# Linear attention beside a SiLU feed-forward: another trigger for one input load, and another order of four transfers and two matmul blocks

## The chip, the cores and the metric

The kernel runs on one core of a Trainium2 chip. The metric is the device time of one execution in microseconds (us). TensorE does the matmuls, VectorE (DVE in the profile), ScalarE (ACT) and GpSimd (POOL) the elementwise work, SyncE (SP) issues most of the transfers. PSUM, which matmuls write, has eight banks of 512 fp32 columns.

## The reference

One input x of 2048 tokens and 448 channels is normalised. Two branches read the result, and both are added to x.

```python
xn  = layernorm(x)                                    # over 448 channels, eps 1e-5
q, k, v = split(xn @ wqkv)                            # 16 heads of 28
pq, pk  = q @ w_phi, k @ w_phi                        # per head, 28 x 28
phi = lambda p: concat(softmax(p), softmax(-p))       # 56 features per head
kv, z = phi(pk).T @ v, sum(phi(pk), tokens)
o   = phi(pq) @ kv / (phi(pq) @ z + 1e-6)
out = x + o @ wo + silu(xn @ w1) @ w2                 # w1: 448 x 1792, w2: 1792 x 448
```

All inputs are bfloat16.

## The kernel before

**Tiles.** The tokens are 16 tiles of 128. `x_sb` holds x, `RA` the normalised rows (`xn_sb`), and `xnT` their transposes, channels on the partitions. The 448 channels are four pieces of 128 that overlap in part; dense blocks multiply 64 rows at a time, two such matmuls side by side.

**Recording and ordering.** The function does not emit instructions at once. Each operation is recorded with its engine, what it reads and writes, and a name (`_Prog.op`, line 186); the reads and writes give its dependencies. `_Prog.schedule` (line 228) then lays the operations out one engine after the other by estimated times, and `emit_engine` (line 1209) writes each engine's program in that order, with semaphore waits for the dependencies that cross engines. Two things fix orders by hand: `chain(names)` (line 1022) makes every named operation follow the one before it on its engine, and the string `PLAN` (line 361) gives the order of TensorE's blocks.

**The words of PLAN.** `aF5@4` is the first half of layer 1 (ffn1) block 5 in the PSUM banks 4 and 5, `bF5` its second half, after which ScalarE writes silu of the two banks to `hT`. `av4@6` and `bv4` are the halves of the value products of tiles 4 and 5 (`v_block`, line 795); after the second half ScalarE copies the two banks to `vaug`. Blocks F0 to F6 are those of tokens 0 to 511, F7 to F13 of tokens 512 to 1023 (tiles 4 to 7), and so on. `f0@6` and `f1@6` fold `w_phi` into the key weights (`fold_k`, line 672), `ak2`, `bk2` are key products of tiles 2 and 3. A second half also waits until the first half has left TensorE, since both add to the same banks.

**The head.** Tiles 0 to 3 are normalised and transposed on the engines: VectorE's statistics (lines 708, 709), ScalarE's square root (712), VectorE's reciprocal (714) and normalisation (723), TensorE's transposes (541), and copies out of PSUM (547, 551). Tiles 0 and 1 are loaded by SyncE, one DMA each; tiles 2 and 3 by one DMA of ScalarE, which is recorded as `x2`. It reads nothing that another engine makes; line 1036 makes it wait for an operation of GpSimd:

```python
byname["x2"].deps.add(byname["ident"].id)
```

Behind it on ScalarE follow, by the chain in line 1034, a warm activation with its table load and the square roots. GpSimd's first operations are, in order, `ones`, `epst`, `ident` (the identity for the transposes), `neghalf`, `ones4`, the zero fill of `Wp` (the first operation with the name `wp_zero`), a mask, the zero fill of `Wp0` (the second), and more masks and fills. TensorE meanwhile runs 39 matmuls on constants (line 591).

**SyncE's queue.** From tile 4 on a pair of tiles is transposed by one DMA, from `RA` to `xnT` (`xnT_dma5` for tiles 4 and 5, `xnT_dma7` for 6 and 7, and so on, line 731); it waits for VectorE's normalisation of both. Nine further DMA transposes (`wT_dma0` to `wT_dma8`, line 650) bring pieces of `wqkv`; `f0` and `f1` read the pieces 4 to 8. `x8` and `x12` load tiles 8 to 11 and 12 to 15. SyncE issues in order, by the chain in line 1072, so an issue that waits holds back all behind it.

Of the kernel before, what the change touches and what calls it, by code (L numbers as in the profile page):

```python
# [140 lines left out]
class _Prog:  # L141
# [86 lines left out]
    def schedule(self, stalls=()):  # L228
# [53 lines left out]
        while done < n:  # L282
# [75 lines left out]
TAIL = {"act": 110.0, "dve": 85.0, "pool": 45.0}  # L358
SIGNAL = {("act", "pe"): 60.0, ("act", "dve"): 40.0, ("dve", "pe"): 100.0, ("dve", "sp"): 30.0, ("dve", "dve"): 34.0,
          ("pool", "pe"): 100.0}  # L360
PLAN = """r0 aF3@4 r2 r1 bF3 aF6@0 aF4@6 bF6 bF4 aF5@4 av2@2 av0@0 bv2 bF5 bv0 av4@6 aF10@2 bv4 aF9@0 bF10 f0@6 bF9 aF12@4 aF7@2
aF11@0 f1@6 bF11 bF7 bF12 aF8@0 ak2@6 bF8 bk2 av12@2 av8@4 ak0@0 bv8 bv12 bk0 av10@6 aF22@4 bv10 bF22 aF17@2 aF14@0 av14@6
bF17 bv14 aF18@4 bF14 aF27@6 ak4@2 bF27 bF18 bk4 ak6@0 av6@6 ak8@4 bv6 bk8 bk6 ak12@2 aF25@6 bk12 bF25 aY0@45 aY0 aF21@0
aF23@2 bF21 ak14@6 bF23 bY0 g0@1 bk14 bY0 aF13@0 aF19@2 bF13 aF24@6 aF20@4 bF19 bF20 bF24 ak10@0 g1@3 bk10 K0 K6 K4 K12
# [6 lines left out]
def bass_parallel_sum__linear_kernel_hedgehog__dense_activation_silu__prompt_kernel(  # L371
# [37 lines left out]
    with es:  # L409
        def sb(name, shape, dt):  # L410
            return es.enter_context(nc.sbuf_tensor(name, shape, dt))
# [60 lines left out]
        ident = sb("ident", [128, 128], BF16)  # L472
# [33 lines left out]
        P = _Prog()  # L506
# [83 lines left out]
        for i in range(39):  # L590
            o = P.op("pe", 107.0, lambda e: e.matmul(banks[3][:, 0:128], unit, unit, start=True, stop=True),
                 reads=[], writes=[banks[3][:, 0:128]], name="warm", mode=128)
# [306 lines left out]

        early = {int(w[2]) for w in PLAN.split() if w[1:2] == "Y"}  # L900
        ob_cnt = [0]
# [120 lines left out]
        def chain(names):  # L1022
            byname = {o.name: o for o in P.ops}
            for a, b in zip(names, names[1:]):
                byname[b].odeps.add(byname[a].id)
                byname[b].odeps -= byname[b].deps
# [6 lines left out]
        chain("bnst0 bnag0 bnst1 rstd0 bnag1 xn0 rstd1 xn1 bnst2 bnag2 bnst3 rstd2 xn2 bnag3 rstd3 xn3 ev3".split())  # L1033
        chain("x2 warm_act ve0 ve1 ev0a ev0 ev1a ve2 ev1 ve3 ev2a ev2 silu_table".split())
        byname = {o.name: o for o in P.ops}
        byname["x2"].deps.add(byname["ident"].id)
        byname["x2"].xfer, byname["x2"].lat = 0.0, 2800.0
        fold_loads()

# [29 lines left out]

        for t in range(8, NT):  # L1070
            ln_tile(t)
        chain("x8 wT_dma4 wT_dma5 wT_dma6 x12 wT_dma7 xnT_dma5 xnT_dma7 wT_dma8 xnT_dma9 xnT_dma11 xnT_dma13 xnT_dma15 wT_dma0 wT_dma1 wT_dma2 wT_dma3 w2 "
              "wo0 wor0 wo1 wor1".split())
        memset(phq[:, :, :, KP:128], 0.0, 400, "phq0")
        for t in (0, NEK):
# [28 lines left out]

        for word in PLAN.split():
            n0 = len(P.ops)
# [81 lines left out]
        for e in ("pe", "act", "dve", "pool"):  # L1188
            cnt = 0
            for oid in order[e]:  # L1190
                o = ops[oid]
# [4 lines left out]
        for e in ENGINES:  # L1196
            for oid in order[e]:
                o = ops[oid]
# [76 lines left out]
```

## Time and profile before

| | |
|---|---|
| median of three runs | 144.99 us (144.57, 144.99, 145.91) |
| profiled execution | 145.19 us, of which the span of instructions is 143.9 us |
| granted TensorE clock, mean | 1.0 |
| TensorE busy | 140.4 us in 1969 matmuls |
| VectorE, ScalarE, GpSimd busy | 90.3, 79.7 and 75.3 us |
| moved by DMA | 17.59 MB in 45,044 packets, mean 122 GB/s |

The span is the time from the first to the last instruction of the program; the profiled execution's time holds 1.3 us around it. Times within the profile count from the span's start. The profile's page gives busy times, the span in 40 slices of 3.6 us, and the chain of work that ended last; the timeline lists instructions in order of time with start and duration, where several of one kind are merged into one row. "L524" is line 524 of the kernel, the helper that records every matmul, so matmuls are told apart by their tiles; `phT` is also the place where w1 lies at first, so `psum<-xnT,phT` is a layer 1 matmul, `psum<-wv,xnT` a value product, and `psum<-BD,wT` or `psum<-BD,Y_sb` a fold (the transposed weight pieces lie in `Y_sb` and `wT8`). Rows with a q behind the engine ("ACTq", "SPq") are DMAs that it issues, with the time that the issue took, not the transfer.

### The profile page before, as it was taken

To read this page: it belongs to the slowest core of one execution; us is meant where nothing else is said; L and a number is where in the kernel's file an instruction comes from. 1 tells how busy PE (TensorE), PEld (TensorE's weight loads), DVE (VectorE), ACT (ScalarE), POOL (GpSimd) and SP (SyncE) were. 2 spreads that over 40 slices of the span, in tenths; PEclk is the share of its full clock that TensorE was granted. 3 is DMA by queue.
4 is the path that set the end of the run, shared out by engine and by line. 5 is a ranking of instruction groups with operands and counts; after the bars stand their busy time and mean duration, and the time that the engine had idled before them with its cause. 6 is when DMAs were issued, how large, how long until landed. Compare 5 with 4: busy or idle time off the path is not lost.

```text
span 143.9 us, 4560 instructions
## 1 busy us (share of the span) xinstructions
PE 140.4 (98%) x1969; PEld 83.1 (58%) x1969; DVE 90.3 (63%) x194; ACT 79.7 (55%) x98; POOL 75.3 (52%) x95
## 2 busy tenths in 40 slices
PE   7799999999999999999999999999999999999994
PEld 7794444445444544477677656555555556555773
DVE  1879897700760069939049999957977564265533
ACT  4577866479996999889787949237440000000000
POOL 8808667430196008799944999993495700000000
PEclk9999999999999999999999999999999999999999
DMA  4999999555990000000000058959789998825422
GB/s 129 315 324 300 270 191 97 100 106 82 322 328 8 0 2 5 0 0 5 0 5 5 0 98 168 143 110 108 152 158 146 234 214 151 141 40 112 162 95 64
DMA packets 45044, 17.59 MB, mean 122 GB/s; under 512 B 36944, under 2 KB 44640, under 8 KB 45024
## 3 DMA queue, kind: packets, MB, share of 16 engines
q1 hardware_dynamic: 42448, 15.25, 53.3%
q10 hardware_dynamic: 2448, 2.02, 5.0%
q8 instruction: 15, 0.25, 0.7%
q0 software_dynamic: 128, 0.03, 0.1%
q14 instruction: 5, 0.04, 0.1%
HBM read 6.57 MB, written 1.84 MB: 58 GB/s over the span
## 4 chain that ended last, share of the span: by engine, by line
PE 94%; DMA 2%; DVE 1%; SPq 0%; ACT 0%; issue 0%
PE psum L524 94%; DMA x_sb<-in_A_x_dram 2%; PE psum L541 1%; DVE st L708 0%; SPq L561 0%; DVE RA L723 0%; DVE x_sb L1009 0%; ACT ve L712 0%; DVE rstd L714 0%; DVE mv L709 0%
## 5 line engine op out<-in xcount | busy, mean ns | idle before, releaser
L524 PE MATMUL psum<-xnT,phT 64*128 64x512 bf16 (+1 forms) x428 | 46.6, 350 | 0.0
L524 PE MATMUL psum<-w_sb,hT 64*128 64x448 bf16 (+4 forms) x455 | 46.0, 341 | 0.0
L843 DVE TENSOR_REDUCE Rec<-Ek_sb 128x32 f32<-128x896 bf16 (+1 forms) x20 | 24.6, 1257 | 18.6 <-ACT Ek_sb L547 18.6
L524 PEld LDWEIGHTS psum<-w_sb,hT 64*128 64x128 bf16 (+1 forms) x455 | 23.8, 94 | 17.2 <-issue 0.2
L547 ACT ACTIVATE hT<-psum 128x1024 bf16<-128x1024 f32 x28 | 27.6, 1024 | 10.8 <-PE psum L524 10.8
L524 PEld LDWEIGHTS psum<-xnT,phT 64*128 64x128 bf16 (+1 forms) x428 | 22.6, 95 | 17.6 <-ACT vaug L547 0.7
L880 POOL TENSOR_TENSOR RA<-Ek_sb,Rec 128x896 bf16<-128x896 bf16 x16 | 27.0, 1723 | 6.0 <-DVE Rec L844 4.4
L524 PE MATMUL psum<-Wqk,xnT 64*128 64x432 bf16 x224 | 24.4, 343 | 0.0
L547 ACT ACTIVATE Ek_sb<-psum 128x864 bf16<-128x864 f32 x24 | 20.4, 916 | 6.4 <-PE psum L524 5.5
L853 POOL TENSOR_TENSOR Ek_sb<-Ek_sb,Rec 128x896 bf16<-128x896 bf16 x8 | 13.4, 1698 | 16.3 <-DVE Rec L844 16.3
L524 PEld LDWEIGHTS psum<-Wqk,xnT 64*128 64x128 bf16 x224 | 11.1, 94 | 8.2 <-ACT hT L547 0.4
L547 ACT ACT_TABLE_LOAD x11 | 14.1, 1283 | 2.7 <-POOL Wp L554 1.8
L853 POOL TENSOR_TENSOR phT<-phT,Rec 128x896 bf16<-128x896 bf16 x8 | 13.4, 1699 | 1.7 <-issue 0.9
L524 PE MATMUL psum<-wv,xnT 64*128 64x448 bf16 x112 | 12.4, 349 | 0.0
L708 DVE BATCH_NORM_STATS2 st<-x_sb 128x6 f32<-128x448 bf16 x16 | 9.7, 604 | 3.5 <-DMA x_sb<-in_A_x_dram 3.5
L524 PE MATMUL psum<-wo_sb,vaug 64*128 64x448 bf16 (+2 forms) x102 | 11.3, 338 | 0.0
L1009 DVE TENSOR_TENSOR x_sb<-psum,x_sb 128x448 bf16<-128x448 f32 (+2 forms) x13 | 7.2, 583 | 5.5 <-PE psum L524 5.5
L988 DVE TENSOR_TENSOR vaug<-psum,rden 128x448 bf16<-128x448 f32 x16 | 9.3, 620 | 0.0
L723 DVE TENSOR_SCALAR RA<-x_sb,mv,rstd 128x384 bf16<-128x384 bf16 (+2 forms) x28 | 8.8, 352 | 0.8 <-POOL rstd L719 0.6
L843 DVE TENSOR_REDUCE Rec<-phT 128x64 f32<-128x1792 bf16 x4 | 8.0, 1990 | 1.9 <-ACT phT L547 1.8
L844 DVE RECIPROCAL Rec<-Rec 128x32 f32<-128x32 f32 (+1 forms) x24 | 8.8, 396 | 0.2
L547 ACT ACTIVATE vaug<-psum 128x896 bf16<-128x896 f32 x8 | 7.5, 949 | 2.4 <-PE psum L524 2.4
(60 smaller groups left out, 106.6 us busy)
## 6 DMA issues: line engine op xcount, KB each, us to landing
out_dram<-x_sb ACTq DMA_DIRECT2D x15, 112.0 KB, 2.4
w_sb<-in_B_w_dram SPq DMA_DIRECT2D x1, 1568.0 KB, 7.8
x_sb<-in_A_x_dram SPq DMA_DIRECT2D x3, 448.0 KB, 5.6
wo_sb<-in_A_wo_dram SPq DMA_DIRECT2D x2, 336.0 KB, 7.4
phT<-in_B_w_dram SPq DMA_DIRECT2D x3, 192.0 KB, 5.0
phT<-in_B_w_dram SPq DMA_DIRECT2D x1, 576.0 KB, 6.3
phT<-in_B_w_dram SPq DMA_DIRECT2D x2, 256.0 KB, 3.8
wv<-in_A_wqkv_dram SPq DMA_DIRECT2D x1, 336.0 KB, 6.7
```

The lines of the kernel that those rows point to most:

```text
L524: r = e.matmul(dst, lhsT, rhs, start=st, stop=sp, skip_group_check=True)
L541: r = e.transpose(dst, src, ident[:])
L547: P.op("act", d_act(n), lambda e: e.activation(dst, src, func, scale=scale), reads=[src], writes=[dst], table=table, name=name, **keys)
L708: P.op("dve", 590, lambda e: e.bn_stats(st6[:, t, :], xs), reads=[xs], writes=[st6[:, t, :]], name=f"bnst{t}", okeys_w=["ln"])
L723: P.op("dve", dur, lambda e: e.tensor_scalar(dst, x_sb[:, t, c0:c1], mv[:, t, 0:1], rstd[:, t:t + 1], ALU.subtract, ALU.mult), reads=[xs, ...
L843: P.op("dve", 50 + 967 * n, lambda e: e.tensor_reduce(R2, E4, AXL.X, ALU.add), reads=[E4], writes=[R2], name=f"Ssum_{tag}")
L844: P.op("dve", 135 + 210 * n, lambda e: e.reciprocal(R2, R2), reads=[R2], writes=[R2], name="Rrec")
L853: P.op("pool", 1700, lambda e: e.tensor_tensor(E3, E3, Rk[:, :, None].broadcast_to([128, 32, DH]), ALU.mult), reads=[E3, Rk], writes=[E3], ...
L880: P.op("pool", 1700, lambda e: e.tensor_tensor(dst, Eq, Rq.rearrange("p (c j) -> p c j", c=CC)[:, :, :, None].broadcast_to([128, CC, 4, DH ...
L988: P.op("dve", 620, lambda e: e.tensor_tensor(o4, U4[:, :, :, 0:DH], rden4[:, :, :, None].broadcast_to([128, CC, 2, DH]), ALU.mult), reads= ...
L1009: P.op("dve", d_dve(cs.stop - cs.start), lambda e: e.tensor_tensor(res[:, cs], ob, addend[:, cs], ALU.add), reads=[ob, addend[:, cs]], wri ...
```

## The change

There are three edits.

1. `x2`, ScalarE's load of tiles 2 and 3, waits for the first `wp_zero`, the fill of `Wp`, instead of `ident`.
2. On SyncE `xnT_dma5` comes ahead of `x12`, and `xnT_dma7` ahead of `wT_dma7`. The five issues were `x12 wT_dma7 xnT_dma5 xnT_dma7 wT_dma8` and become `xnT_dma5 x12 xnT_dma7 wT_dma7 wT_dma8`.
3. On TensorE the order `bv0 av4 aF10 bv4 aF9` becomes `av4 bv0 bv4 aF10 aF9`. The banks stay the same.

```diff
-PLAN = """... av2@2 av0@0 bv2 bF5 bv0 av4@6 aF10@2 bv4 aF9@0 bF10 f0@6 ...
+PLAN = """... av2@2 av0@0 bv2 bF5 av4@6 bv0 bv4 aF10@2 aF9@0 bF10 f0@6 ...
...
-        byname["x2"].deps.add(byname["ident"].id)
+        byname["x2"].deps.add(next(o.id for o in P.ops if o.name == "wp_zero"))
...
-        chain("x8 wT_dma4 wT_dma5 wT_dma6 x12 wT_dma7 xnT_dma5 xnT_dma7 wT_dma8 xnT_dma9 ...
+        chain("x8 wT_dma4 wT_dma5 wT_dma6 xnT_dma5 x12 xnT_dma7 wT_dma7 wT_dma8 xnT_dma9 ...
```

In the built program the order of VectorE's, ScalarE's and GpSimd's instructions is the same as before; SyncE's differs in the five issues named and TensorE's in the blocks named. The numbers of instructions and of bytes are unchanged.

## The prediction

> **What bounds the kernel now.** I read the page's busy shares first, then its slices, then the chain of work that ended last, and then the timeline around the places that the change touches.
>
> ```profile
> PE 140.4 (98%) x1969; PEld 83.1 (58%) x1969; DVE 90.3 (63%) x194; ACT 79.7 (55%) x98; POOL 75.3 (52%) x95
> ...
> PE   7799999999999999999999999999999999999994
> ```
>
> TensorE is busy in 98% of the span, and only the first two slices and the last one fall short. A busy TensorE need not be at its peak, so I took the distance between the starts of successive matmuls from the timeline. From 9.3 us on, two 64-row matmuls of 512 columns start every 0.213 us, of 448 columns every 0.186, of 432 every 0.179, and up to 60 us hardly a distance is longer than these by over 0.01 us. So TensorE is fed without a break there, and nothing that only reorders its work there can win time. Time can be won before 9.3 us, and lost anywhere. The chain, in order of time, shows what the head hangs on:
>
> ```profile
> 1.28 3.00 DMA x_sb<-in_A_x_dram
> 4.28 0.02 issue
> 4.30 0.63 DVE st L708
> 4.92 0.06 DVE rstd L714
> ...
> 5.70 0.41 DVE RA L723
> 6.11 0.04 issue
> 6.16 0.40 PE psum L541 x4
> ...
> 9.43 132.57 PE psum L524 x1849
> ```
>
> The reader is to see that the end of the span hangs on the landing of x tile 1. It is issued at 1.28 us and lands at 4.28, its statistics start at 4.30, its normalisation ends at 6.11, its transposes run at 6.16, and from there TensorE goes on to the end. The head has only the latency of that one load to give.
>
> **Part 1: the load of x 2 and 3 waits for the fill of Wp instead of ident.** In the timeline GpSimd's ident ends at 1.38 and ScalarE issues at once; the fill of Wp runs from 1.41 to 1.60.
>
> ```profile
> 1.09 0.29 POOL L564 TENSOR_SCALAR_AFFINE_SELECT ident<-ones_bf 128x128 bf16<-128x128 bf16 x1
> ...
> 1.41 0.19 POOL L554 MEMSET Wp<- 128x112 bf16 x1
> 1.41 0.38 ACTq L561 DMA_DIRECT2D x_sb<-in_A_x_dram  x1
> ...
> 1.82 1.28 ACT L547 ACT_TABLE_LOAD   x1 [1.82 <-POOL Wp L554]
> ```
>
> The issue moves by 1.60 - 1.38 = 0.22 us, to about 1.63. Queued behind it on ScalarE are the table load (1.82 to 3.10), the warm activation (3.11 to 3.32) and the first square root at 3.78. The last has been idle for 0.46 us, so a shift of 0.22 is covered and 0.24 is left. Tiles 2 and 3 land at 4.46 now (3.1 us after the issue by the page) and their statistics start at 6.02: the cover is 1.56 us, so their own lateness costs nothing.
>
> The gain is in x 1. The packet records of the trace show tile 1 almost through (218.7 of the 229.4 KB of tiles 0 and 1) at 3.0 us, but its last twelve packets of 896 bytes come between 3.07 and 3.82 us, each about 0.11 us after the one before on what must be the same DMA engine. Alone, such packets take 0.041 us; those of x 2 and 3, 1792 bytes, take 0.074, and they run from 2.76 to 3.94. 0.041 + 0.074 = 0.115: the laggards alternate with the ScalarE load. If that load starts 0.22 us later, a lagging engine moves 0.22 / 0.041 = 5 packets in that stretch instead of 2, and three steps of 0.11 us fall away: x 1 would land 0.33 us earlier.
>
> Against it stands one row: ScalarE's load of x starts 1.35 us after its issue, while a lone store issued by ScalarE late in the kernel (141.34 us) starts after 0.84. So it already stood in line for some 0.5 us, which can swallow 0.22. The ends are therefore 0 and a bound from above. That bound comes from the next load in line: the second piece of w1 lands at 6.22 and is first read at 6.84, so not much over 0.5 us of shift finds its data. A loss is excluded by the covers just named. Between 0 and 0.5 I take 0.2, a little below the mean of 0 and 0.33, and pass it on in full: every step from the statistics of tile 1 to the first ffn matmul waits for the one before by 0.02 to 0.1 us.
>
> The Trainium skill ("DMA: Bandwidth & Descriptors", Queues, rings and completion order) has each DMA engine go round its queue rows a packet of some 9 to 17 descriptors at a time. By that the 8 rows of x 1 on an engine would leave as one packet, and a load that comes 0.22 us later would not split them at all; the sum would then have the whole bound, 0.5. The trace's single steps of 0.11 us speak against it.
>
> **Part 2: SyncE's order.** The five issues concerned run now without a wait: x 12 at 12.07 (1.32 us long), weight transpose 7 at 13.44 (1.32), the transposes of tiles 4/5 at 14.81 (1.31) and 6/7 at 16.16 (1.65), weight transpose 8 at 17.85 (1.26). With 4/5 in front, SyncE must wait for VectorE's normalisation of tile 5, which ends at 13.50 (the pair at 12.90, 0.60 us long). So the five end at 13.52 + 1.31 + 1.32 + 1.65 + 1.32 + 1.26 + four steps of 0.04 = 20.5 instead of 19.1, less the 0.2 of the head. One by one:
> - Tiles 4/5 go out at 13.5 instead of 14.81 and have x 12 and a weight transpose less ahead of them. They land at 18.85 now and earlier after.
> - Tiles 6/7 start at about 16.2 as now and land after 4.1 us, at 20.3; they are read first by the layer 1 block of these tokens, at 21.06 now (0.85 us after the landing) and 0.74 us later in the new order.
> - x 12 is issued at 14.9. Now it lands 5.6 us after its issue, at 17.6, behind weight transposes that land up to 16.46; so after, between 18.5 and 20.5. Its statistics start at 19.57. VectorE could stand up to 1 us, and with it tile 11, whose transposes have 7 us until TensorE reads them.
> - Weight transposes 7 and 8 go out at 17.9 and 19.2 instead of 13.44 and 17.85. The last lands 3.1 us after its issue now (at 20.97), so at 22.3. The fold of the key weights reads it at 23.98, 23.8 with the head's gain: 1.5 us of cover are left of 3.0.
> - The transposes of 8/9 and 10/11 behind them slip by up to 1.4 us and are not read before 30 us; those of 12 to 15 wait for VectorE, and w2 behind them is read at 54.7, having landed at 41.9.
>
> All of part 2 costs nothing while these covers hold.
>
> **Part 3: the value products of tiles 4/5 ahead.** The same matmuls stand in another order:
>
> ```profile
> 19.74 1.49 PE L524 MATMUL psum<-wv,xnT 64*128 64x448 bf16 x14
> 21.06 0.81 PE L524 MATMUL psum<-xnT,phT 64*128 64x512 bf16 x6
> 21.71 0.92 PE L524 MATMUL psum<-wv,xnT 64*128 64x448 bf16 x8
> 22.47 1.67 PE L524 MATMUL psum<-xnT,phT 64*128 64x512 bf16 x14
> ```
>
> First half of 4/5 (3 x 0.186), second of 0/1 (4 x 0.186), second of 4/5, then layer 1 (3 x 0.213) and its next block at 22.42, against 22.47 now: the sum is unchanged. That next block takes the banks of values 0/1, whose matmuls now end 0.56 us later. Their ScalarE copy would run from about 21.26 (0.40 us after the last pair starts, as with the copy at 22.68) to 22.20: 0.2 us of cover is left. If it is gone, it costs at most 0.1.
>
> **The sum.** -0.2 (head) + 0 + 0 against the profiled execution's 145.19 us (span 143.9 and 1.3 around it) is 145.0. That execution lies 0.2 above the median of the three runs, 144.99; carried to the median, the forecast is 144.8.
>
> **Rivals.**
> 1. The ScalarE load stands in its line of 0.5 us anyway, and x 1 lands as before. For it: 1.35 against 0.84 us. The time is 145.0; the rest is as forecast.
> 2. Slower: the last weight transpose lands after the fold wants it. The trace has an instruction fetch of 16 KB at 22.02 us lasting 1.13 us, and from 22.6 to 23.75 the packet records show hardly a transpose packet; the transposes of 8/9, in flight there, took 5.1 us to land. If weight transpose 8 falls into that stretch, it lands at 19.25 + 5.1 = 24.3 against 23.8: 0.5 us of stall, less the head's 0.2, gives 145.3. It decides from a landing 4.5 us after the issue on. Against it: at 3.1 us it is through before 22.6.
> 3. By the arbitration rule's mechanism x 1 goes clear of the other load: -0.5, 144.5.
> 4. A wait that I have not priced, by one of the blocks with little cover, of over 1.5 us: 146.5 or more.
>
> **How the numbers follow.** The forecast has 0.55, rival 1 0.25, rival 2 0.1, rival 3 0.05, and rival 4 0.05. A change of 1% is 1.45 us; the three runs alone spread from 144.57 to 145.91, so none of the first four cases can be told from no change by that bound: within 1% is 0.92, slower 0.06, faster 0.02, the last for spread alone. The range goes from the best case less the spread below the median (144.5 - 0.4 = 144.1) to rival 2 with a little of the spread above (145.5).
>
> **What would show it.** In the new profile the ScalarE issue should stand at 1.63, the load of x 1 in the chain should be shorter than 3.00 us, and the first dense matmul, now at 6.39, earlier by 0.2. The transposes of 4/5 should be issued at 13.3 and the weight transposes end by 20.4, with the fold directly behind the matmul before it. The step that I trust least is the head's 0.2; the step that could turn the sign is the fold's weight transpose: a gap on TensorE before the fold's matmuls would make me wrong.

## The result, and the profile after

The median is 145.54 us (22 runs, 144.78 to 146.07), against 145.20 (22 runs, 144.49 to 145.91) of the kernel before beside it. The ratio is 1.0034 [1.0021, 1.0048]: slower by a third of a per cent, within the 1% of "no change" but not by chance, and on the other side of the forecast. The profiled execution took 145.52 us, its span 144.3, against 145.19 and 143.9. Now and then an execution of any kernel here takes over 1.5% longer than its fastest; below, the medians are over all runs and the ratios leave these out.

The page of the kernel after, the lines that answer to those shown of before, and the row of the layer 1 matmuls (its last field is the idle time ahead of such matmuls, and what ended it):

```profile
PE 140.4 (97%) x1969; PEld 83.1 (58%) x1969; DVE 90.4 (63%) x194; ACT 79.6 (55%) x98; POOL 75.2 (52%) x95
...
PE   7999998999999999999999999999999999999994
...
PE 83%; DMA 10%; SPq 4%; DVE 1%; issue 1%
...
L524 PE MATMUL psum<-xnT,phT 64*128 64x512 bf16 (+1 forms) x428 | 46.5, 350 | 0.8 <-DMA xnT<-RA 0.8
```

TensorE's work is the same 140.4 us. But one slice in the middle of the run of nines is an 8: the seventh, 21.6 to 25.2 us. And the layer 1 matmuls have waited 0.8 us for a transfer of transposes. The same row of before:

```profile
L524 PE MATMUL psum<-xnT,phT 64*128 64x512 bf16 (+1 forms) x428 | 46.6, 350 | 0.0
```

The chain that ended last no longer starts with x tile 1. In order of time, from the kernel after:

```profile
7.46 7.82 DMA x_sb<-in_A_x_dram
15.28 0.02 issue
15.30 0.64 DVE st L708
15.94 0.02 issue
15.96 0.07 DVE mv L709
16.03 6.04 DMA xnT<-RA
22.07 0.14 issue
22.21 120.13 PE psum L524 x1714
```

Read from below: TensorE goes on to the end from 22.21 without a break; it was released by the transposes of tiles 6/7, issued at 16.03 and landed 6.04 us later. (The step from VectorE's `mv` at 15.96 to the issue is inferred; SyncE's own row shows that the issue followed x 12's.) The place on TensorE's timeline (start, duration, what, and the idle time that the profile gives):

```profile
0.84 4.05 PE L591 MATMUL psum<-const-bfloat16-1.0 128*128 128x128 bf16 x39 [0.84 <-PEq L1260]
4.87 0.40 PE L541 MATMUL psum<-ident,RA 128*128 128x128 bf16 x4
5.54 0.40 PE L541 MATMUL psum<-ident,RA 128*128 128x128 bf16 x4 [0.28 <-DVE RA L723]
5.78 1.55 PE L524 MATMUL psum<-xnT,phT 128*128 128x128 bf16 x24
...
19.14 2.26 PE L524 MATMUL psum<-wv,xnT 64*128 64x448 bf16 x22
22.21 2.33 PE L524 MATMUL psum<-xnT,phT 64*128 64x512 bf16 x20 [0.81 <-DMA xnT<-RA]
24.36 0.19 PE L524 MATMUL psum<-BD,Y_sb 64*128 64x56 bf16 x1
```

The first dense matmul starts at 5.78, 0.61 us ahead of that of before:

```profile
6.39 1.51 PE L524 MATMUL psum<-xnT,phT 128*128 128x128 bf16 x24
```

Comparing start by start (the n-th matmul after against the n-th before), that lead holds until 21.2 us. There the layer 1 block of tiles 4 to 7 should follow the value products; it starts at 22.21, and from there on the kernel is 0.40 us behind, 0.34 at the end. (The 0.81 of the row is less than these 1.0 us, as the ends of matmuls are modelled; I go by starts.) So 0.6 was won in the head and 1.0 lost in one wait; 145.52 - 145.19 = 0.33 is the difference of the two within 0.1.

SyncE's rows around it:

```profile
13.16 2.20 SPq L631 DMA_TRANSPOSE xnT<-RA  x1
15.41 0.58 SPq L561 DMA_DIRECT2D x_sb<-in_A_x_dram  x1
16.03 1.24 SPq L631 DMA_TRANSPOSE xnT<-RA  x1
17.31 2.58 SPq L631 DMA_TRANSPOSE Y_sb<-in_A_wqkv_dram  x2
```

The transposes of 6/7 were issued at 16.03, as forecast (16.2). Their landing was to be at 20.3, 4.1 us later; it came at 22.07. What delays them is seen in the view of the transfers between 12 and 26 us, cut in 40 slices of 0.35 us (GB/s moved in each), after:

```profile
GB/s 386 402 352 297 193 86 44 40 35 278 243 247 245 290 203 51 205 379 329 356 159 283 281 232 94 15 8 9 156 185 204 46 7 238 280 287 237 187 218 211
...
q8 instruction: 1, 0.02, 0.5%
```

and before:

```profile
GB/s 399 393 360 282 201 69 31 18 267 228 379 215 492 328 244 281 289 281 290 290 161 63 142 114 173 209 208 155 104 217 110 15 10 10 263 95 0 157 217 206
...
q8 instruction: 1, 0.02, 0.5%
```

Three slices move almost nothing: 15, 8, 9 from 20.75 to 21.8 us after, and 15, 10, 10 from 22.85 to 23.9 before. Each stretch begins 0.7 to 0.8 us after the start of the window's one transfer of the queue q8, an instruction fetch of 16 KB: at 20.09 us (1.06 long) after, at 22.02 (1.13 long) before. Before, it met transposes that are read 7 us later. After, it met the tail of 6/7.

Not every low slice is this fetch. The one of after at 13.75 to 15.15 us (86, 44, 40, 35) begins a microsecond after the first fetch of q8 (11.64 to 12.72) has ended, and 46 and 7, from 22.85 on, follow 8 KB on the queue q14 at 22.19. Nor did the first fetch stop the loads that were in flight then (386, 402, 352). But in each of the eighteen profiles of this study the packets fall under 60 GB/s for a microsecond or more within 1.2 us of the second fetch's start, wherever that lies between 19.70 and 23.36.

### The profile page after: what moved, and what is told of

Read it like the earlier page. It is cut to its first block, busy times and chain, and to the rows that moved or that the text cites. A ratio compares the mean times of both kernels' runs of the same rounds, so it can differ in the third digit from the quotient of the medians.

```text
span 144.3 us, 4560 instructions
## 1 busy us (share of the span) xinstructions
PE 140.4 (97%) x1969; PEld 83.1 (58%) x1969; DVE 90.4 (63%) x194; ACT 79.6 (55%) x98; POOL 75.2 (52%) x95
## 4 chain that ended last, share of the span: by engine, by line
PE 83%; DMA 10%; SPq 4%; DVE 1%; issue 1%
PE psum L524 83%; DMA x_sb<-in_A_x_dram 5%; SPq L561 4%; DMA xnT<-RA 4%; DVE st L708 0%; DVE x_sb L1009 0%; DVE mv L709 0%
## 5 line engine op out<-in xcount | busy, mean ns | idle before, releaser
L524 PEld LDWEIGHTS psum<-wv,xnT 64*128 64x128 bf16 x112 | 5.8, 94 | 5.0
```

Source lines behind the costliest of these rows:

```text
L524: r = e.matmul(dst, lhsT, rhs, start=st, stop=sp, skip_group_check=True)
```

## The experiments

The ratios are to the kernel before on the same chip, with 95% intervals; each is of 12 runs, but for a single execution of the kernel before. They are not quotients of the two medians: on the chip of the first three runs here, where the kernel before scatters up to 146.74 us, they come out lower (144.94 / 145.10 would be 0.9989, not 0.9970). "Earlier" and "lead" compare the start of a matmul with that of the same number in the first profile of before.

Three theories were written down first: A, SyncE's new order makes 6/7 late, and the head's gain is real; B, the new trigger of x 2/3 makes 6/7 late; C, the head's gain is chance. Later A was split: A1, x 12's 448 KB in front are enough; A2, x 12 only takes the cover away, and what holds the tail of 6/7 is the instruction fetch at 20 us.

### Each edit alone, and pairs

**The first edit alone** (the kernel before with the new trigger):

```diff
-        byname["x2"].deps.add(byname["ident"].id)
+        byname["x2"].deps.add(next(o.id for o in P.ops if o.name == "wp_zero"))
```

> The first edit alone: ScalarE's load waits for the fill of Wp, SyncE and TensorE keep the order of before. Theory A (the wait for tiles 6/7 comes from SyncE's new order, which puts the 448 KB of x 12 directly ahead of them; the head's gain is real): 0.3 to 0.6 us faster than before, with the first dense matmul at 5.8 us instead of 6.4 and at most 0.3 us of wait for tiles 6/7, which TensorE then asks for at 20.45. Theory B (the wait comes from the head: TensorE asks earlier while all loads come some 0.4 us later, so 6/7 would be late in any order): no gain or up to 0.4 us slower, with the wait still there. Theory C (the head's gain was chance in one profile): 0 within 0.1 us.

144.94 against 145.10, ratio 0.9970 [0.9939, 1.0000]. x 1 landed at 3.29, 6/7 at 20.64 with the fetch at 22.30, and the end came 0.33 us earlier. B falls: the trigger alone makes nothing late. The gain is at the edge of its interval.

**The change without the first edit** (the reverse of that diff in the kernel after):

> The second and third edits without the first: ScalarE's load waits for ident as before. Theory A: TensorE reaches layer 1 of tiles 4 to 7 at 21.8 us, the transposes of 6/7 land at about 22.0 as in the changed kernel, so a wait of 0.1 to 0.4 us and a time 0.1 to 0.9 us above before, since the head's 0.6 is not there to pay for it. Theory B: no wait, the same time as before within 0.1 us.

145.77 against 145.10, ratio 1.0027 [0.9993, 1.0060]. The wait is there without the trigger: 6/7 landed at 22.26, and the fetch began at 20.19. But x 1 landed at 3.53 with the old trigger too, and the head was 0.47 us earlier. So part of the head's gain is chance, as C says. The span lost a further 0.25 us at 77 us, where the kv products wait; that is not explained.

**The first and third edits, SyncE's order as before:**

```diff
-        chain("x8 wT_dma4 wT_dma5 wT_dma6 xnT_dma5 x12 xnT_dma7 wT_dma7 wT_dma8 ...
+        chain("x8 wT_dma4 wT_dma5 wT_dma6 x12 wT_dma7 xnT_dma5 xnT_dma7 wT_dma8 ...
```

> The first and third edits; SyncE keeps its order of before, with x 12 and weight transpose 7 ahead of tiles 4/5. Theory A: no wait for 6/7 (they land at about 20.2 to 20.5, asked for at 21.2), the whole head's gain stays: 0.4 to 0.7 us faster than before. A wait of up to 0.3 us could stand at the value products of tiles 4/5, which are asked for at 19.1 and land at 18.9 in before. Theory B: 6/7 still late, 0 to 0.4 us slower than before.

144.82 against 145.10, ratio 0.9961 [0.9932, 0.9989], the only gain of the study that is clear by its interval. Its profiled execution, 145.42, was the slowest of the twelve and shows another near-tie: the value products of 4/5, now ahead, waited 0.7 us (to 19.70) for the transposes of 4/5, which in SyncE's old order land at 19.56. The same kernel on another chip:

> The first and third edits once more, on the same chip as the changed kernel: 0.3 to 0.7 us below before, 0.6 to 1.0 below the changed kernel; 4/5 landing at 18.9 to 19.6 and a wait of up to 0.5 us for them.

144.86 against 144.82, ratio 0.9998 [0.9977, 1.0019]. The gain was not repeated. This time the profiled execution (145.80, again the slowest of its twelve) waited 0.66 us at 13.59 for the last piece of w1, which landed at 13.46 instead of 12.03.

**x 12 behind 6/7,** the other two edits as in the change:

```diff
-        chain("x8 wT_dma4 wT_dma5 wT_dma6 xnT_dma5 x12 xnT_dma7 wT_dma7 wT_dma8 ...
+        chain("x8 wT_dma4 wT_dma5 wT_dma6 xnT_dma5 xnT_dma7 x12 wT_dma7 wT_dma8 ...
```

> All three edits, but x 12 is issued behind both transposes (order 4/5, 6/7, x 12, weight transposes 7 and 8). Theory A: tiles 6/7 land by about 19.5 us, the wait of 0.8 us is gone, 0.4 to 0.7 us faster than before; x 12 comes later and VectorE stands at its statistics by another 1 us without cost. Theory B: the wait stays, 0 to 0.4 us slower than before.

145.05 against 145.10, ratio 0.9974 [0.9942, 1.0007]. 6/7 landed at 18.55 and TensorE did not wait for them; the end came 0.54 us earlier in the profile. The cost went to x 12, which landed at 20.73; VectorE's timeline has

```profile
20.76 0.63 DVE L708 BATCH_NORM_STATS2 st<-x_sb 128x6 f32<-128x448 bf16 x1 [1.23 <-DMA x_sb<-in_A_x_dram]
```

and some 0.2 us of it reached TensorE, where the second fold (26.51) had to wait for VectorE's subtraction of the first (line 701). The order is the cause of the wait, then, but this run cannot say by what: both A1 and A2 let it go when x 12 moves.

### x 12's bytes or the fetch

**SyncE's order alone** (the kernel before with the second edit):

> The second edit alone (SyncE's new order, with x 12 between the transposes of 4/5 and 6/7; TensorE's order and ScalarE's load as before). Theory A1 (x 12's 448 KB ahead of 6/7 make them late by themselves): 6/7 land at 21.5 to 22.1 us, TensorE asks at 20.5 to 21.1, so it waits 0.5 to 1.5 us, and the time is 0.4 to 1.0 us above before. Theory A2 (x 12 ahead only takes the cover away, and the instruction fetch at 20.1 us, seen in both kernels that have the new orders of SyncE and TensorE together, holds the last part of 6/7): with TensorE's old order the fetch comes at 22 us, 6/7 land at 20.6 to 20.9, a wait of at most 0.3 us, and the time within 0.3 us of before.

144.94 against 145.14, ratio 0.9997 [0.9979, 1.0014]. **The first and second edits:**

> The first and second edits, TensorE's order as before. As the run with the second edit alone, by A1 0.3 to 1.0 us above before with a wait of 0.8 to 1.5 us for 6/7; by A2 between 0.3 below and 0.2 above before, with the fetch at about 22 us and a wait of at most 0.4 us.

145.27 against 145.14, ratio 1.0021 [0.9996, 1.0045]. These two have the same order on SyncE and the same on TensorE. TensorE's timelines, of the order alone:

```profile
19.85 1.49 PE L524 MATMUL psum<-wv,xnT 64*128 64x448 bf16 x14
21.17 0.81 PE L524 MATMUL psum<-xnT,phT 64*128 64x512 bf16 x6
```

and with the trigger:

```profile
19.16 1.49 PE L524 MATMUL psum<-wv,xnT 64*128 64x448 bf16 x14
22.00 0.82 PE L524 MATMUL psum<-xnT,phT 64*128 64x512 bf16 x6 [1.35 <-DMA xnT<-RA]
```

With the order alone the layer 1 block follows directly: 6/7 landed at 20.30, with x 12 ahead of them at 19.31, and the fetch began at 21.98. With the trigger too, the block waits 1.5 us: the fetch began at 19.70, and 6/7 landed at 21.86. A1 falls here, since x 12's bytes lie ahead of 6/7 in both. What I had put down for A2, that the fetch stays at 22 us with TensorE's old order, was wrong as well; where the fetch starts is not set by that order. That second profile was the slowest of its twelve runs, so the wait need not be in each of them.

**x 12 much earlier,** right behind x 8:

```diff
-        chain("x8 wT_dma4 wT_dma5 wT_dma6 xnT_dma5 x12 xnT_dma7 wT_dma7 wT_dma8 ...
+        chain("x8 x12 wT_dma4 wT_dma5 wT_dma6 xnT_dma5 xnT_dma7 wT_dma7 wT_dma8 ...
```

> All three edits, but x 12 is issued right behind x 8, ahead of the weight transposes, so that nothing large lies ahead of the tile transposes. Both theories: 4/5 land by 18.3 and 6/7 by 19.5 us, no wait for either, VectorE does not stand at x 12, and the fold has its operands: 0.3 to 0.6 us faster than before. If another wait shows, it is at the fold (weight transpose 8 lands after 23.5).

145.31 against 145.14, ratio 1.0014 [0.9991, 1.0037]. 6/7 landed at 20.70 without a wait, but everything behind x 12 slipped, and the fetch, at 22.73, hit the next tie:

```profile
21.30 2.32 PE L524 MATMUL psum<-xnT,phT 64*128 64x512 bf16 x20
24.94 0.18 PE L524 MATMUL psum<-BD,Y_sb 64*128 64x56 bf16 x1 [1.32 <-POOL rstd L719]
```

The profile puts the idle time before the fold down to GpSimd's `rstd`; but in the kernel after the fold ran at 24.36, before the same `rstd` ended at 24.82. By the transfers of the trace, weight transpose 8 landed at 24.81, 0.13 us ahead of the fold. This is rival 2 of the prediction, in another kernel.

**The kernel before again,** one execution beside these:

> The kernel before, unchanged, for another look at the head. If the first edit makes the head's gain, x tile 1 lands at 4.0 to 4.4 us again and the first dense matmul starts at 6.3 to 6.5. If the late tile 1 was chance of the first profile, it lands at 3.3 to 3.7 us as in the run without the first edit, and the matmul starts at 5.8 to 6.0.

144.85 us. x 1 landed at 3.80, between the two cases, and the first dense matmul came 0.31 earlier than in the first profile of the same kernel; 6/7 landed at 20.27, and the fetch began at 22.00. So the head of the profile that I had predicted from was late for its kind.

### Moving the fetch

The idea is that the fetch follows the count of instructions that TensorE has read. The 39 warm-up matmuls of 128 columns stand at its head; with 20 of 256 columns instead, it is to ask for its code 19 matmuls later, at nearly the same warm-up time. Beside the kernel after, on one chip.

**The kernel after again:**

> The changed kernel once more, beside the next three. The instruction fetch at 19.7 to 20.3 us, tiles 6/7 landing at 21.8 to 22.3, a wait of 0.6 to 1.2 us on TensorE behind a head 0.4 to 0.7 us earlier than in the first profile of before; 0.3 to 0.5 us slower than before in the median.

145.55 against 144.82, ratio 1.0053 [1.0032, 1.0075]. 6/7 landed at 22.05 and TensorE waited 0.6 us for them; the lead of the head was only 0.25, as x 1 landed at 3.99. **The kernel after with fewer and wider warm-up matmuls:**

```diff
-            o = P.op("pe", 107.0, lambda e: e.matmul(banks[3][:, 0:128], unit, unit, start=True, stop=True),
+            o = P.op("pe", 107.0, lambda e, i=i: None if i % 2 else e.matmul(banks[3][:, 0:256], unit, nc.const_aps.tensor(1.0, [128, 256], BF16), start=True, stop=True),
```

> The changed kernel with its 39 warm-up matmuls of 128 columns replaced by 20 of 256, so that TensorE runs 19 instructions fewer before its first real one and its program is fetched 19 matmuls later in the work; all else is as in the changed kernel (every later fetch moves too, by some 2 us). Theory A2 (the fetch that falls on tiles 6/7 makes the wait): the fetch now at 20.1 us comes at 21.5 to 22.5, 6/7 land at 20.2 to 20.8, no wait over 0.1 us for them, and the time is 0.3 to 0.6 us below before. Theory A1 (x 12 ahead of 6/7 makes them late by itself): 6/7 land at 21.8 or later again, and the time stays 0.2 to 0.5 us above before.

144.83 against 144.82, ratio 0.9998 [0.9977, 1.0019]. The two intervals do not meet: the loss is gone, with SyncE's order, x 12 in front and the order of TensorE's blocks untouched. The timelines, of the kernel after again:

```profile
19.49 2.24 PE L524 MATMUL psum<-wv,xnT 64*128 64x448 bf16 x22
22.19 2.33 PE L524 MATMUL psum<-xnT,phT 64*128 64x512 bf16 x20 [0.46 <-DMA xnT<-RA]
```

of the other:

```profile
19.42 2.24 PE L524 MATMUL psum<-wv,xnT 64*128 64x448 bf16 x22
21.50 2.32 PE L524 MATMUL psum<-xnT,phT 64*128 64x512 bf16 x20
23.66 0.19 PE L524 MATMUL psum<-BD,wT 64*128 64x56 bf16 x1
```

and its transfers between 12 and 26 us:

```profile
GB/s 443 428 377 266 190 40 15 15 222 234 245 287 250 257 41 164 297 396 332 223 220 283 267 144 160 100 219 207 208 161 96 31 204 4 3 10 32 291 269 227
```

The fetch began at 22.63 instead of 19.92, the empty slices (4, 3, 10, 32) lie at 23.55 to 24.95, and 6/7 landed at 20.36 instead of 22.05. x 12 landed at 19.37, so its bytes were as much in the way as before.

The control is **the kernel before with the same warm-up:**

> The control: the kernel before with the 20 warm-up matmuls of 256 columns that mended the changed kernel. Both theories: the second fetch at 22 to 23 us, no wait for tiles 4 to 7, the time of before within 0.2 us. If it is 0.4 us or more faster than before, the longer warm-up matmuls are worth something by themselves and the mended kernel proves less than it seemed to.

144.97 against 145.07, ratio 1.0001 [0.9981, 1.0021]. The other warm-up by itself gains nothing; the fetch was at 22.53, only half a microsecond later than in before.

The other direction was tried on **the kernel before, with 58 warm-up matmuls of 86 columns:**

```diff
-            o = P.op("pe", 107.0, lambda e: e.matmul(banks[3][:, 0:128], unit, unit, start=True, stop=True),
+            o = P.op("pe", 107.0, lambda e, i=i: [e.matmul(banks[3][:, 0:86], unit, unit[:, 0:86], start=True, stop=True) for _ in range(2 if i < 19 else 1)][-1],
```

> The kernel before with 58 warm-up matmuls of 86 columns instead of 39 of 128: the same warm-up time, but TensorE's instruction fetches are asked for 19 matmuls earlier in the work, the second at about 18.0 to 18.5 us. Theory A2 (a fetch that meets a tile transpose in flight holds it 1 to 2 us, in any order): the fetch at 18 to 19.5 us, 4/5 land after 19.5 and 6/7 after 20.8 us, TensorE waits 0.2 to 1.0 us for one of them, 0.2 to 0.8 us slower than before. If only SyncE's new order is to blame (A1): no wait, the time of before within 0.15 us.

145.37 against 145.07, ratio 1.0018 [0.9996, 1.0040]. The second fetch did not come at 18 us but at 23.36, and it cost nothing there: the expectation missed. The profile's 0.6 us came from a wait for the last piece of w1, which landed at 13.81:

```profile
11.68 1.67 PE L524 MATMUL psum<-xnT,phT 64*128 64x512 bf16 x14
13.94 2.33 PE L524 MATMUL psum<-xnT,phT 64*128 64x512 bf16 x20 [0.59 <-DMA phT<-in_B_w_dram]
```

Whether the first fetch, at 11.45, had a part in that is not shown: it started at 11.40 to 11.48 in four other profiles too, and there the piece landed at 11.65 to 12.38.

### Looking for a better order

**x 12 first, then 4/5 and 6/7,** the other two edits as in the change:

```diff
-        chain("x8 wT_dma4 wT_dma5 wT_dma6 xnT_dma5 x12 xnT_dma7 wT_dma7 wT_dma8 ...
+        chain("x8 wT_dma4 wT_dma5 wT_dma6 x12 xnT_dma5 xnT_dma7 wT_dma7 wT_dma8 ...
```

> The first and third edits with another order on SyncE: x 12 stays first, as before, then the transposes of 4/5 and 6/7, then weight transposes 7 and 8. Issuing x 12 fills the time in which SyncE would wait for tile 5. Both theories: 4/5 land at about 18.6, 6/7 at 19.5 to 20.0, ahead of a fetch at 20 us or later, no wait for either; 0.4 to 0.7 us faster than before, unless weight transpose 8 is caught by a fetch and the fold waits for it (then up to 1 us slower in those executions).

144.88 against 144.82, ratio 1.0001 [0.9982, 1.0020]. No wait for 6/7 (landed at 19.92), 0.3 us for weight transpose 8 (landed at 23.44, fold at 23.58), and 0.43 earlier at the end of the profile, which the medians do not show.

**That order with the fetch moved as well:**

> The order with x 12 first on SyncE, then 4/5, 6/7 and weight transposes 7 and 8, with the first and third edits and the 20 warm-up matmuls of 256 columns. If the fetch is what eats the head's gain, it comes at 22 to 23 us, weight transpose 8 lands by 22, there is no wait from 6 us to the end, and the time is 0.2 to 0.5 us below before (0.15 to 0.35%). If the gain is eaten elsewhere or was not there, 0 within 0.15 us.

145.28 against 144.96, ratio 1.0026 [1.0001, 1.0050]. Nothing won: in its profile the lead was 0.52 us at the last transpose of tile 1 and 0.31 at the first dense matmul, at 6.08, where the first piece of w1 had landed at 5.95; it was down to 0.08 at 6.76, where the second piece, landed at 6.71, was waited for. The fetch was at 21.91, and weight transpose 8, landed at 23.93, held the fold for another 0.13. **The first edit alone, again:**

> The first edit alone, again. Tile 1 lands at 3.3 to 4.0 us, the first dense matmul 0.2 to 0.6 us earlier than in the first profile of before. If the head's gain reaches the end, 0.2 to 0.4 us faster than before; if the looks at before with a quick head are the rule, 0 within 0.15 us.

144.90 against 145.07, ratio 0.9999 [0.9983, 1.0014]. x 1 landed at 3.37, and 0.53 us were won in the head, of which 0.33 was left at the end: the block that reads 6/7 (landed at 20.59) came early enough now to wait 0.2 us for them, at 20.73. No version here has a gain on which two chips agree.

## Why the prediction was wrong

**The step that failed** is in part 2: "Tiles 6/7 start at about 16.2 as now and land after 4.1 us, at 20.3". The issue was right (16.03); the flight took 6.04 us and the landing was at 22.07, against a first use that the head's gain had brought to about 21.2. In the sum, part 2 stood at 0, with a cover of 0.85 + 0.74 - 0.2 = 1.4 us for 6/7; it cost 1.0. I had given the transposes the flight time of the old order. That time held in the new order as well when the fetch was elsewhere (15.70 to 20.30 with SyncE's order alone, and 20.36 with the fetch moved): x 12 in front was not the mistake. The mistake was to take the time of the fetch, 22.02, as fixed.

| profile | fetch starts, us | 6/7 land, us | wait for 6/7, us |
|---|---|---|---|
| before; before again | 22.02; 22.00 | 20.21; 20.27 | none |
| SyncE's order alone | 21.98 | 20.30 | none |
| after, other warm-up | 22.63 | 20.36 | none |
| after; after again | 20.09; 19.92 | 22.07; 22.05 | 1.0; 0.6 |
| without the first edit | 20.19 | 22.26 | 1.0 |
| first and second edits | 19.70 | 21.86 | 1.5 |

**Rival 2** had the mechanism, an instruction fetch that catches a transfer with little cover, but at the wrong transfer and the wrong time, and at half the price (0.5 us, where the wait took 1.0). Its 145.3 lies nearer to the 145.54 than the forecast of 144.8 does. I looked at which transfer moves into the stretch at 22.6 to 23.75, and did not ask whether the stretch moves.

**The head** was right in its sign and too small: 0.61 us in the profile against 0.2. Two things were mixed in it. Over the profiles of this study x 1 landed at 4.28, 3.53, 4.38, 3.80, 3.97 and 3.87 with the old trigger, and with the new one at 3.29 to 3.44 in eleven profiles and at 3.99 in one (the kernel after again): 0.57 us earlier in the mean (3.40 against 3.97), and the profile that I worked from was one of the two latest of its kind. Rival 1's premise held for the front of the ScalarE load alone: its first packet came at 2.71 to 2.81 with the new trigger (twelve profiles) and at 2.58 to 2.90 with the old (six). But half of its 128 packets had started by 3.50 to 3.78 with the new trigger and by 3.21 to 3.48 with the old, 0.31 us later in the mean; and x 1's last packet started at 3.03 in the kernel after, against 3.82. So the bulk of the load did come later, as part 1 needs. By part 1's own working 0.31 us are 7 packets instead of 2 or 3, so some 0.5 us; that is an estimate, and no run tests it. (Two slips of the working: 0.2 lies above the mean of 0 and 0.33, not below it, and the distances of matmuls given as 0.213, 0.186 and 0.179 us are 0.216, 0.189 and 0.182 in the trace. Neither decides anything.) The Trainium skill's rule of whole packets per row ("DMA: Bandwidth & Descriptors", Queues, rings and completion order), rival 3, is neither shown nor ruled out by this gain, which came near its 0.5 too.

**The bound of the head** that I had named, the second piece of w1, did decide in one run, that with x 12 first and the fetch moved. With the first edit alone another bound decided, which I had not seen: TensorE's own pace. Its matmuls of 128 columns start every 0.107 us at first and every 0.056 later, while the profile gives a granted clock of 1.0 for both stretches, and the change comes at different times from profile to profile: at 4.42 us in the kernel after and 4.74 in before, ahead of the dense matmuls, but at 6.55 with the first edit alone. The first 24 dense matmuls of that run (1.55 us long in the kernel after):

```profile
5.91 1.81 PE L524 MATMUL psum<-xnT,phT 128*128 128x128 bf16 x24
```

Of its lead of 0.65 us at the transposes of tile 1, 0.17 was left at 6.6, with the second piece of w1 landed at 6.45 and not waited for; a wait of before for tile 2 gave some of it back, to 0.37. In the second run of that kernel the change came at 6.00 and 0.53 stayed. Over the profiles with the warm-up of before it came between 3.46 and 6.55; what sets it is not shown.

**The other covers of part 2.** VectorE hardly stood at x 12 (landed at 19.55, read at 19.58, under 0.1 us later than it could have been) and it cost nothing, as said; x 12 at 20.73 did cost 0.2. The fold's cover was not the 1.5 us that I worked out: weight transpose 8 landed at 23.75, not 22.3, and the fold read it at 24.36. Without the wait for 6/7 the fold would have come 1.0 us sooner and met it. **Part 3** cost nothing, as forecast: no wait was seen at the block that follows the copy of values 0/1, nor in the runs with part 3 where 6/7 were in time (21.14 and 21.50 us).

**What stays open** is why the second fetch starts at 19.7 to 20.2 us in the profiles with the wait and at 20.6 to 23.4 in the others. In the run with x 12 behind 6/7 it started at 20.75, right after x 12 had landed at 20.73, so a fetch may have to stand behind transfers that read device memory; but I found no rule that fits all the profiles, no run tested this one, and the run that was to place the fetch earlier did not.

Counting matmuls narrows it. In the fourteen profiles with 39 warm-up matmuls the third fetch starts when 341 to 349 matmuls have started, the fourth at 469 to 477, 120 to 134 further on. The second starts at 215 to 219 in the four with the wait, 122 to 132 ahead of the third, and at 223 to 245 in the others. So with the wait it seems to come on its count, and elsewhere late. With 20 warm-up matmuls it came at 224 in the kernel after and in before, 128 ahead of the third; with 58 at 260, only 84 ahead. And of the five profiles with SyncE's new order and the old warm-up, the four with the early fetch have a TensorE that leads by 0.25 to 0.6 us at 20 us, and the fifth, with the fetch at 21.98, one that trails by 0.11. The gain of the head may so have helped to bring the loss. This is read from profiles; no run tested it.

The first and second edits together show the limit: in their profile the wait was 1.5 us, while the median of their twelve runs is only 0.2% above before, so the fetch may not fall into this place in every execution of that kernel.

## What to carry to other kernels

Where the bound engine has no gaps, a reordering of transfers is worth what the least cover of a reader allows; before that cover is trusted, look for what else is transferred in the window, instruction fetches too, and ask whether it moves when the work before it does. A landing taken from one profile is one draw: here one load, its neighbour's trigger unchanged, landed between 3.5 and 4.4 us, a spread larger than the gain that was looked for. A gain won ahead of several loads, each with half a microsecond to spare, is easily spent at the next one that comes late.

## What the runs showed of the hardware

- One instruction fetch of 16 KB, 1.06 to 1.49 us long, was followed by a near stop of the transposes in flight, from over 200 GB/s to under 35 for three or four slices of 0.35 us, beginning 0.7 to 0.9 us after its own start (three kernels shown above). A transfer caught in it landed 1.6 to 2 us later: 22.05 against 20.36 side by side.
- With 20 warm-up matmuls of twice the width in place of 39, the fetch of the kernel after came at 22.63 instead of 19.92 and the kernel took 0.5% less time, with the rest of the work unchanged. Fewer instructions ahead of it are not enough to place it: the same change moved it from 22.02 to 22.53 in before, and 58 narrower ones brought it to 23.36, where 18 was expected.
- TensorE's first matmuls ran at half pace, 0.107 us for 128 columns instead of 0.056, until 3.46 us in one profile and 6.55 in another, after the same warm-up.
- Executions of one kernel differ by 1.3 to 1.4 us from fastest to slowest (144.49 to 145.91 before). The profiles show where: x 1's landing, TensorE's change of pace, the last piece of w1 (11.65 to 13.81), the transposes of 4/5 and 6/7, the fold, and an unexplained 0.25 to 0.3 us at 77 us in three profiles. All but the second and the last are near-ties between a transfer and its reader.
